# Cutting the 576 result columns of three products at column 252 instead of 288, and laying them as one run over two PSUM banks

## The chip, the core and the metric

The kernel runs on one core of a Trainium2 chip. The metric is the device time of one execution in microseconds, lower is better. A core has five engines that work side by side: PE (TensorE: matmuls; its loading of the stationary operand has a row of its own, PEld), DVE (VectorE), ACT (ScalarE), POOL (GpSimd) and SP (SyncE, which here only starts DMAs). PE writes its results to PSUM, a memory of eight banks, each with 512 fp32 columns on 128 partitions. A matmul's results lie within one bank, so 576 columns need at least two matmuls.

## What is computed

Two kinds of block alternate, each twice, over 2048 rows of 576 values: a linear attention, then a layer of 64 experts that each of 32 heads chooses from. Each adds to its input.

```python
x = x + _A_ref(_layernorm(x, axis=-1), A_wqkv, A_wo)
x = x + _B_ref(_layernorm(x, axis=-1), B_w_q, B_k1, B_k2, B_u, B_v)
x = x + _A_ref(_layernorm(x, axis=-1), A_wqkv, A_wo)
x = x + _B_ref(_layernorm(x, axis=-1), B_w_q, B_k1, B_k2, B_u, B_v)
```

`_A_ref` makes q, k and v (`x @ wqkv`, 576 columns each, 32 heads of 18), takes phi(t) = t + 1 for t > 0, else exp(t), plus 1e-6, of q and k, sums phi(k) times v over all rows for each head, multiplies phi(q) with that sum, divides by phi(q) times the sum of phi(k), and multiplies with `wo`. `_B_ref` scores every row for 32 heads against two sets of 8 keys, takes the best of each (one of 64 experts), weighs that expert's row of `v` with the gelu of x times its row of `u`, and sums over the heads.

## The kernel before

**Tiles and layers.** The 2048 rows are 16 tiles of 128. For each of the two layers a *front* makes k, v, q and the state (the sum over all tiles), and a *back* makes the attention's output, the scores, the choice and the experts' output, tile by tile. The back of a tile of layer 0 runs beside the front of an earlier tile of layer 1.

**Precision.** A product in float32r loses low bits, so each operand is split in a high and a low part (`split`, L102; names ending in hi and lo), and a product is the sum of hi x hi, hi x lo and lo x hi. With 576 = 4.5 x 128 contraction rows in five blocks, that is 14 passes (`passes`, L48). Each pass takes two matmuls, one for each part of the 576 result columns: 28 matmuls for one product of a tile.

**The products that the change concerns.**
- `product` (L207, matmul L214) makes k, v and q of a tile: tiles ppk, ppv, ppq. A PSUM tile is 1024 columns, two banks. k and q are cut at `HALF` = 288: columns 0 to 287 go to the first bank from its head, 288 to 575 to the head of the second (column 512). v alone passes `cut=2 * HC` = 252, so that whole groups of seven heads (126 columns) lie together; its parts are 252 and 324 wide, each at the head of a bank.
- `back_out` (L403, matmul L410) makes the attention's output, ppo: 14 passes of two 288-wide matmuls (`out_passes`, L329).
- `exp_out` (L516, matmul L525) makes the experts' output, po: two passes, four matmuls. In the last layer three tiles (10, 11 and 12) begin with an identity matmul that puts the residual into PSUM (`exp_base`, L509, L514).

**Who reads them.** `phi` (L218) reads ppk and ppq twice: exp on ACT (L220) and a max-and-add on DVE (L223), with an in-place step on DVE between them (L221). `residual` (L396, L399) adds ppo or po to the input on DVE and sums the row. For the three tiles with an identity matmul ACT copies po instead (L530). All of them see the two parts through `halves` (L69), a view of 2 x 288 columns with a step of 512.

**Order.** Within `in_order(...)` (L144) the instructions of PE, ACT, DVE and POOL keep the order in which the code issues them, engine by engine. That order is written by hand: a loop over tiles for layer 0's front (L703 on), then lists of pieces (`play`, L674; L760, L779) and a step that is repeated eight times (`step2`, L680). In a list `k1.10` is the next part of layer 1's k for tile 10, `q` and `lq` the q products, `O` the output product, `S` the scores, `po` the experts' output, `sel` the choice on DVE. PSUM tiles come from a ring of four (L66).

Of the kernel before, what the change touches and what calls it, by code (L numbers as in the profile page):

```python
# [15 lines left out]
AF = mybir.ActivationFunctionType  # L16
ALU = mybir.AluOpType
# [4 lines left out]
S, D, H, DH = 2048, 576, 32, 18  # L22
# [2 lines left out]
DK, E, NE = 128, 8, 64  # L25
HC = 7 * DH
HALF = D // 2
EPS_LN = 1e-5
EPS = 1e-6
GELU_C = float(np.sqrt(2.0 / np.pi))  # L30
# [8 lines left out]
def blocks(rem):  # L39

    rows, at = [], 0
    for b in range(NB):
        rows.append((at, b - (b > rem)))
        at += 64 if b == rem else P
    return rows


def passes(rem):  # L48
    rest = [b for b in range(NB) if b != rem]
    return ([("hi", b, "hi") for b in range(NB)] + [("hi", b, "lo") for b in rest]  # L50
            + [("lo", b, "hi") for b in range(NB)])


REM, REM_O = 2, 4
# [3 lines left out]
def network(ctx, tc, x_in, wqkv, wo, wq_t, k_t, u_t, v2, c_mask, c_mask4, c_ident, c_code, c_code1, c_scale, c_shift, out):  # L58
    nc = tc.nc
# [6 lines left out]
    def psum(name):  # L66
        return ps.tile([P, 1024], F32, tag="ps", name=name)

    def halves(t):  # L69
        return t.rearrange("p (b c) -> p b c", b=2)[:, :, :HALF]  # L70


    ident = cp.tile([P, P], F32, name="ident")
# [10 lines left out]
    whi = cp.tile([P, NB, 3 * D], F32R, name="whi")  # L84
    wlo = cp.tile([P, 4, 3 * D], F32R, name="wlo")
# [4 lines left out]
    vmix = cp.tile([P, D], F32R, name="vmix")  # L90
# [67 lines left out]
    def statistics(xt, n, soon=False):  # L158
        st = wk.tile([P, 2, 6], F32, tag="st", name=f"st{n}")
        nc.vector.bn_stats(st[:, 0], xt[:, :HALF])  # L160
        nc.vector.bn_stats(st[:, 1], xt[:, HALF:])
        mv = wk.tile([P, 2], F32, tag="mv", name=f"mv{n}")
        nc.vector.bn_aggr(mv, st.rearrange("p a b -> p (a b)"))  # L163
        rs = wk.tile([P, 2], F32, tag="rs", name=f"rs{n}")
        nc.gpsimd.tensor_scalar(rs[:, 0:1], mv[:, 1:2], EPS_LN, 1.0, op0=ALU.add, op1=ALU.mult)  # L165
        nc.gpsimd.tensor_tensor(rs[:, 0:1], rs[:, 0:1], mhalf, op=ALU.pow)
# [4 lines left out]
    def spread(xt, total, n):  # L171

        m = wk.tile([P, 2], F32, tag="mv", name=f"m{n}")
        nc.gpsimd.tensor_scalar(m[:, 0:1], total, -1.0 / D, 1.0, op0=ALU.mult, op1=ALU.mult)  # L174
        nc.scalar.activation(junk, xt, AF.Square, bias=m[:, 0:1], accum_out=m[:, 1:2])  # L175
        return m

    def layernorm_sum(xt, m, n):
        rs = wk.tile([P, 2], F32, tag="rs", name=f"rs{n}")
        nc.gpsimd.tensor_scalar(rs[:, 0:1], m[:, 1:2], 1.0 / D, EPS_LN, op0=ALU.mult, op1=ALU.add)  # L180
        nc.gpsimd.tensor_tensor(rs[:, 0:1], rs[:, 0:1], mhalf, op=ALU.pow)
        nc.gpsimd.tensor_tensor(rs[:, 1:2], m[:, 0:1], rs[:, 0:1], op=ALU.mult)  # L182
        return normalized(xt, rs, n)
# [20 lines left out]
        split(pt[:, :w], hi.rearrange("p a b -> p (a b)")[:, :w], lo.rearrange("p a b -> p (a b)")[:, :w])  # L204
        return hi, lo

    def product(tt, hi, lo, cols, n, cut=HALF, rem=REM, by_block=False):  # L207

        o = psum(f"pp{n}")
        todo = sorted(passes(rem), key=lambda p: p[1]) if by_block else passes(rem)  # L210
        for i, (a, b, w) in enumerate(todo):
            wb = hi[:, b] if w == "hi" else lo[:, blocks(rem)[b][1]]
            for c0, c1, at in ((0, cut, 0), (cut, D, 512)):
                nc.tensor.matmul(o[:, at:at + c1 - c0], tt[a == "lo"][:, b, :], wb[:, cols + c0:cols + c1],  # L214
                                 start=(i == 0), stop=(i == len(todo) - 1))
        return o

    def phi(p, n):  # L218
        e = wk.tile([P, D], F32, tag="e", name=f"e{n}", bufs=4)
        nc.scalar.activation(e.rearrange("p (b c) -> p b c", b=2), halves(p), AF.Exp)  # L220
        nc.vector.tensor_scalar(e, e, 1.0, EPS, op0=ALU.min, op1=ALU.add)  # L221
        e2 = e.rearrange("p (b c) -> p b c", b=2)
        nc.vector.scalar_tensor_tensor(e2, halves(p), 0.0, e2, op0=ALU.max, op1=ALU.add)  # L223
        return e

    tt = {}
# [9 lines left out]
    def front_k(l, t):  # L236
        k = product(tt["f", l, t], whi, wlo, D, f"k{l}_{t}", by_block=(l == 0 and t == 0))
        yield
        tt["fk", l, t] = phi(k, f"k{l}_{t}")

    def front_v(l, t):
        v = product(tt["f", l, t], whi, wlo, 2 * D, f"v{l}_{t}", cut=2 * HC)
        yield
        vt = v5[t % 2]
        for c, x in ((0, v[:, :2 * HC]), (4, v[:, 512:512 + 2 * HC])):
            nc.scalar.activation(vt[:, c:c + 4, :63], x.rearrange("p (c e) -> p c e", c=4), AF.Copy)  # L246
        yield
        nc.scalar.activation(vt[:, 8:, :36], v[:, 512 + 2 * HC:512 + 2 * HC + 72].rearrange("p (c e) -> p c e", c=2), AF.Copy)

    def front_q(l, t):  # L250
        q = product(tt["f", l, t], whi, wlo, 0, f"q{l}_{t}")
        yield
        fq = phi(q, f"q{l}_{t}")
        nc.sync.dma_start(pq_d[l][t], fq)
# [74 lines left out]
    def out_passes():  # L329
        todo = [(0, b, ohi[:, b], HC if b < 4 else P) for b in range(NB)]  # L330
        todo += [(0, b, olo[:, b], HC) for b in range(4)]
        todo += [(1, b, ohi[:, b], HC) for b in range(4)]
        return todo + [(1, 4, olo[:, 4], 112)]

    def state_fold(l, b):
# [3 lines left out]
        for h in range(2):  # L339
            nc.tensor.matmul(m[:c, h * 512:h * 512 + HALF], kvb[:n, b * HC:b * HC + c], wob[l][b][:n, h * HALF:(h + 1) * HALF],  # L340
                             start=True, stop=True)
# [54 lines left out]
    def residual(p, xt, n, tag):  # L396
        y = wk.tile([P, D], F32, tag=tag, name=f"{tag}{n}", bufs=BUFS[tag])
        total = wk.tile([P, 1], F32, tag="sum", name=f"sum{tag}{n}")
        nc.vector.scalar_tensor_tensor(y.rearrange("p (b c) -> p b c", b=2), halves(p), 0.0,  # L399
                                       xt.rearrange("p (b c) -> p b c", b=2), op0=ALU.add, op1=ALU.add, accum_out=total)  # L400
        return y, total

    def back_out(l, t):  # L403
        n = f"{l}_{t}"
        hl = tt.pop(("oT", l, t))
        p = psum("ppo" + n)
        todo = sorted(out_passes(), key=lambda x: x[1]) if t == 0 else out_passes()
        for i, (a, b, w, r) in enumerate(todo):
            for h in range(2):
                nc.tensor.matmul(p[:, h * 512:h * 512 + HALF], hl[a][:r, b], w[:r, h * HALF:(h + 1) * HALF],  # L410
                                 start=(i == 0), stop=(i == len(todo) - 1))
        yield
        x1, total = residual(p, xs.pop(("a", l, t)), n, "x1")
        xs["b", l, t] = x1
        yield
        m = spread(x1, total, "b" + n)
        yield
        ys["b", l, t] = layernorm_sum(x1, m, "b" + n)
# [90 lines left out]
    def exp_base(l, t):  # L509

        p = tt["base", l, t] = psum(f"po{l}_{t}")
        x1 = xs.pop(("b", l, t))
        for b in range(2):
            nc.tensor.matmul(p[:, b * 512:b * 512 + HALF], ident, x1[:, b * HALF:(b + 1) * HALF], start=True, stop=False)  # L514

    def exp_out(l, t):  # L516
        n = f"{l}_{t}"
        c = tt.pop(("c", l, t))
        p = tt.pop(("base", l, t), None)
        based = p is not None  # L520
        if not based:
            p = psum("po" + n)
        for i in range(2):
            for b in range(2):
                nc.tensor.matmul(p[:, b * 512:b * 512 + HALF], c[i], vmix[:, b * HALF:(b + 1) * HALF],  # L525
                                 start=(i == 0 and not based), stop=(i == 1))
        yield
        if based:
            x2 = wk.tile([P, D], F32, tag="x2", name=f"x2{n}", bufs=BUFS["x2"])
            nc.scalar.activation(x2.rearrange("p (b c) -> p b c", b=2), halves(p), AF.Copy)  # L530
        else:
            x2, total = residual(p, xs.pop(("b", l, t)), n, "x2")
        if l == 0:
            nc.sync.dma_start(x_d[t], x2)
            yield
            m = spread(x2, total, "f" + n)
            yield
            ys["f", 1, t] = layernorm_sum(x2, m, "f" + n)
        else:
            nc.sync.dma_start(out[t * P:(t + 1) * P, :], x2)  # L540
# [125 lines left out]
    keep, rl, lq, ldx, ldq = front_keep, late_load, late_q, back_x, back_pq  # L666
    fl, ln, lv, sv = first_load, first_ln, load_vu, split_vu
    k, v, q, fT, st = front_k, front_v, front_q, front_T, front_state
    wl, mk, zs, M = wo_load, state_mask, state_sum, state_fold
    ld, num, oT, O = back_load, back_scale, back_oT, back_out  # L670
# [32 lines left out]
    with in_order(*ALL):  # L703
        x0, x1 = xs.pop(("f", 0)), xs.pop(("f", 1))
# [156 lines left out]
```

## Time and profile before

| what | value |
|---|---|
| runs | 750.99, 752.0 and 753.03 us; median 752.0 |
| profiled execution | span of 750.2 us from the first instruction to the last; what lies around the span is not in it, and no other time is given for this execution |
| PE | 731.1 us busy, 5672 matmuls |
| PEld | 681.5 us, as many weight loads |
| DVE | 460.1 us |
| ACT | 289.6 us |
| POOL | 197.5 us |
| granted TensorE clock | 0.996 of full speed on the mean |
| HBM | 55.12 MB read, 23.56 MB written, 105 GB/s over the span |

A matmul's row in the profile spans from its start to its modelled end, and one begins before the one ahead has ended. So the cost of a matmul in a stream is read from the distance between starts, not from its length. A row such as `41.83 1.46 PE L214 MATMUL ppv<-whi,thif ... x10` of the timeline is ten matmuls, merged, the first of which starts 41.83 us after the span's start. In the busy table of stretches, each engine has its busy time and the number of its instructions; behind them stand the granted clock, the share of the DMA engines and GB/s.

### The profile page before, as it was taken

The numbers are of one execution on the slowest core, as the hardware profiler recorded it, in microseconds if no ns is written. First come the engines' busy times: TensorE is split into PE (matmuls) and PEld (weight loads), VectorE is DVE, ScalarE is ACT, GpSimd is POOL, SyncE is SP. The second block draws the span as 40 slices with busy tenths as digits, with TensorE's granted clock in tenths as the row PEclk, the third lists the DMA queues.
The fourth block names the chain that finished last, engine by engine and source line by source line (L and its number), as shares of the span: only waits on it lengthen the run. The fifth ranks groups of instructions, "written<-read, shape, count | busy, mean of one in ns | idle before, by whom it ended". The sixth has DMA issues, their size and how long they took to land. (4 is left out here: it accounts for less than half of the span.)

```text
span 750.2 us, 14647 instructions
## 1 busy us (share of the span) xinstructions
PE 731.1 (97%) x5672; PEld 681.5 (91%) x5672; DVE 460.1 (61%) x1006; ACT 289.6 (39%) x588; POOL 197.5 (26%) x541
## 2 busy tenths in 40 slices
PE   7999999999999999999999999999999999999995
PEld 5999989999998889999999999999899999999984
DVE  4632342324236886666666666563366899899986
ACT  4422232232324544444444444452233333444343
POOL 2110001001003543333333333130033334533431
PEclk9999999999999999999999999999999999999999
DMA  9726446631120322222222212222624323121101
GB/s 267 253 98 235 175 165 227 223 118 50 48 64 32 111 99 71 95 85 90 102 103 88 83 69 86 80 71 68 176 87 119 103 83 116 31 87 41 48 33 64
DMA packets 52471, 79.64 MB, mean 106 GB/s; under 512 B 5617, under 2 KB 22513, under 8 KB 52401
## 3 DMA queue, kind: packets, MB, share of 16 engines
q1 hardware_dynamic: 52400, 78.70, 32.0%
q8 instruction: 45, 0.74, 0.4%
q14 instruction: 26, 0.20, 0.1%
HBM read 55.12 MB, written 23.56 MB: 105 GB/s over the span
## 5 line engine op out<-in xcount | busy, mean ns | idle before, releaser
L221 DVE TENSOR_SCALAR ek<-ek 128x576 f32<-128x576 f32 x32 | 15.1, 472 | 81.7 <-ACT ek L220 81.7
L214 PE MATMUL ppk<-whi,thif 128*128 128x288 f32 x320 | 51.0, 304 | 2.3 <-ACT thif L104 2.2
L214 PEld LDWEIGHTS ppk<-whi,thif 128*128 128x128 f32 x320 | 44.9, 191 | 6.7 <-issue 3.3
L410 PE MATMUL ppo<-ohi,thio 126*128 126x288 f32 (+1 forms) x320 | 50.7, 301 | 0.1
L214 PE MATMUL ppk<-whi,tlof 128*128 128x288 f32 x320 | 49.2, 299 | 0.3 <-DVE tlof L105 0.3
L165 POOL TENSOR_SCALAR rsf<-mvf 128x1 f32<-128x1 f32 x16 | 3.1, 192 | 173.4 <-DVE mvf L163 173.3
L221 DVE TENSOR_SCALAR eq<-eq 128x576 f32<-128x576 f32 x32 | 15.6, 489 | 53.8 <-ACT eq L220 53.8
L214 PE MATMUL ppv<-whi,thif 128*128 128x252 f32 x320 | 47.4, 295 | 0.1
L214 PE MATMUL ppv<-whi,tlof 128*128 128x252 f32 x320 | 46.9, 293 | 0.0
L189 ACT ACTIVATE yb<-x,rsb 128x640 f32<-128x640 f32 x32 | 29.6, 923 | 43.4 <-POOL rsb L182 43.3
L441 PE MATMUL pps<-shi,thib 128*128 128x512 f32 x160 | 43.9, 404 | 2.0 <-ACT thib L104 2.0
L214 PEld LDWEIGHTS ppk<-whi,tlof 128*128 128x128 f32 x320 | 45.4, 191 | 0.5 <-DVE tlof L105 0.5
L410 PEld LDWEIGHTS ppo<-ohi,thio 126*128 126x128 f32 (+1 forms) x320 | 44.9, 189 | 1.0 <-DVE eq L223 0.3
L214 PEld LDWEIGHTS ppv<-whi,thif 128*128 128x128 f32 x320 | 43.7, 188 | 0.4 <-ACT thif L104 0.3
L214 PEld LDWEIGHTS ppv<-whi,tlof 128*128 128x128 f32 x320 | 43.9, 188 | 0.0
L175 ACT ACTIVATE junk<-x,mb 128x576 bf16<-128x576 f32 x32 | 24.7, 771 | 49.6 <-POOL mb L174 46.3
L441 PE MATMUL pps<-shi,tlob 128*128 128x512 f32 x160 | 42.7, 397 | 0.0
L246 ACT ACTIVATE v<-ppv 128x252 f32<-128x252 f32 x64 | 20.9, 378 | 53.3 <-PE ppv L214 53.3
L214 PE MATMUL ppq<-whi 128*128 128x288 f32 x260 | 39.8, 299 | 0.6 <-DVE eq L223 0.6
L214 PE MATMUL ppk<-wlo,thif 128*128 128x288 f32 x256 | 40.3, 299 | 0.0
L410 PE MATMUL ppo<-olo,thio 126*128 126x288 f32 x256 | 40.3, 296 | 0.0
L410 PE MATMUL ppo<-ohi,tloo 126*128 126x288 f32 x256 | 40.3, 296 | 0.0
(155 smaller groups left out, 1749.0 us busy)
## 6 DMA issues: line engine op xcount, KB each, us to landing
fold<-in_wq_t SPq DMA_DIRECT2D x64, 288.0 KB, 5.0
whi<-hl_d SPq DMA_DIRECT2D x26, 320.0 KB, 3.1
pq_d<-eq SPq DMA_DIRECT2D x19, 288.0 KB, 2.1
pq<-pq_d SPq DMA_DIRECT2D x19, 288.0 KB, 2.9
xf<-in_x SPq DMA_DIRECT2D x16, 288.0 KB
x<-in_x SPq DMA_DIRECT2D x16, 288.0 KB, 2.7
x_d<-x SPq DMA_DIRECT2D x16, 288.0 KB, 3.2
x<-x_d SPq DMA_DIRECT2D x16, 288.0 KB, 2.7
```

The costliest lines, as they stand in the source:

```text
L165: nc.gpsimd.tensor_scalar(rs[:, 0:1], mv[:, 1:2], EPS_LN, 1.0, op0=ALU.add, op1=ALU.mult)
L175: nc.scalar.activation(junk, xt, AF.Square, bias=m[:, 0:1], accum_out=m[:, 1:2])
L189: nc.scalar.activation(y, x2, AF.Identity, scale=rs[:, 0:1], bias=rs[:, 1:2])
L214: nc.tensor.matmul(o[:, at:at + c1 - c0], tt[a == "lo"][:, b, :], wb[:, cols + c0:cols + c1], start=(i == 0), stop=(i == len(todo) - 1))
L221: nc.vector.tensor_scalar(e, e, 1.0, EPS, op0=ALU.min, op1=ALU.add)
L246: nc.scalar.activation(vt[:, c:c + 4, :63], x.rearrange("p (c e) -> p c e", c=4), AF.Copy)
L410: nc.tensor.matmul(p[:, h * 512:h * 512 + HALF], hl[a][:r, b], w[:r, h * HALF:(h + 1) * HALF], start=(i == 0), stop=(i == len(todo) - 1))
L441: nc.tensor.matmul(p[:, :512], hl[a == "lo"][:, b, :], shi[:, b] if w == "hi" else slo[:, blocks(REM)[b][1]], start=(i == 0), stop=(i == l ...
```

## The change

The parts of k, q, the output product and the experts' output become columns 0 to 251 and 252 to 575, as v's are. The first part is put at columns 260 to 511 of the PSUM tile, at the end of the first bank, and the second at 512, the head of the second bank. So the 576 results are one run from column 260 to 835, and the readers take them as one flat run (`row`) instead of two. v keeps its places (0 and 512). The number of matmuls, weight loads, reads and DMAs and their order on each engine are as before.

```diff
+CUT = 2 * HC
...
+    def row(t):
+        return t[:, 512 - CUT:512 - CUT + D]
+
+    PARTS = (0, CUT, 512 - CUT), (CUT, D, 512)
...
-    def product(tt, hi, lo, cols, n, cut=HALF, rem=REM, by_block=False):
+    def product(tt, hi, lo, cols, n, parts=PARTS, rem=REM, by_block=False):
...
-            for c0, c1, at in ((0, cut, 0), (cut, D, 512)):
+            for c0, c1, at in parts:
                 nc.tensor.matmul(o[:, at:at + c1 - c0], tt[a == "lo"][:, b, :], wb[:, cols + c0:cols + c1],
                                  start=(i == 0), stop=(i == len(todo) - 1))
...
-        nc.scalar.activation(e.rearrange("p (b c) -> p b c", b=2), halves(p), AF.Exp)
+        nc.scalar.activation(e, row(p), AF.Exp)
         nc.vector.tensor_scalar(e, e, 1.0, EPS, op0=ALU.min, op1=ALU.add)
-        e2 = e.rearrange("p (b c) -> p b c", b=2)
-        nc.vector.scalar_tensor_tensor(e2, halves(p), 0.0, e2, op0=ALU.max, op1=ALU.add)
+        nc.vector.scalar_tensor_tensor(e, row(p), 0.0, e, op0=ALU.max, op1=ALU.add)
...
-        v = product(tt["f", l, t], whi, wlo, 2 * D, f"v{l}_{t}", cut=2 * HC)
+        v = product(tt["f", l, t], whi, wlo, 2 * D, f"v{l}_{t}", parts=((0, CUT, 0), (CUT, D, 512)))
...
-        nc.vector.scalar_tensor_tensor(y.rearrange("p (b c) -> p b c", b=2), halves(p), 0.0,
-                                       xt.rearrange("p (b c) -> p b c", b=2), op0=ALU.add, op1=ALU.add, accum_out=total)
+        nc.vector.scalar_tensor_tensor(y, row(p), 0.0, xt, op0=ALU.add, op1=ALU.add, accum_out=total)
...
-            for h in range(2):
-                nc.tensor.matmul(p[:, h * 512:h * 512 + HALF], hl[a][:r, b], w[:r, h * HALF:(h + 1) * HALF],
-                                 start=(i == 0), stop=(i == len(todo) - 1))
+            for c0, c1, at in PARTS:
+                nc.tensor.matmul(p[:, at:at + c1 - c0], hl[a][:r, b], w[:r, c0:c1], start=(i == 0), stop=(i == len(todo) - 1))
...
-        for b in range(2):
-            nc.tensor.matmul(p[:, b * 512:b * 512 + HALF], ident, x1[:, b * HALF:(b + 1) * HALF], start=True, stop=False)
+        for c0, c1, at in PARTS:
+            nc.tensor.matmul(p[:, at:at + c1 - c0], ident, x1[:, c0:c1], start=True, stop=False)
...
-            for b in range(2):
-                nc.tensor.matmul(p[:, b * 512:b * 512 + HALF], c[i], vmix[:, b * HALF:(b + 1) * HALF],
-                                 start=(i == 0 and not based), stop=(i == 1))
+            for c0, c1, at in PARTS:
+                nc.tensor.matmul(p[:, at:at + c1 - c0], c[i], vmix[:, c0:c1], start=(i == 0 and not based), stop=(i == 1))
...
-            nc.scalar.activation(x2.rearrange("p (b c) -> p b c", b=2), halves(p), AF.Copy)
+            nc.scalar.activation(x2, row(p), AF.Copy)
```

## The prediction

> **What bounds the kernel now.** First the head of the page, sections 1 and 2: busy time by engine, then busy tenths in 40 slices, with the TensorE clock that was granted.
>
> ```profile
> span 750.2 us, 14647 instructions
> PE 731.1 (97%) x5672; PEld 681.5 (91%) x5672; DVE 460.1 (61%) x1006; ACT 289.6 (39%) x588; POOL 197.5 (26%) x541
> ...
> PE   7999999999999999999999999999999999999995
> ...
> DVE  4632342324236886666666666563366899899986
> ...
> PEclk9999999999999999999999999999999999999999
> ```
>
> TensorE has work in every slice and full clock in all; VectorE is half idle early and close to full in the last ten slices. The matmul ends are modelled, so a busy PE alone doesn't show a PE at its limit. The question is where it ever waits, and who else is full there. The busy table over five stretches (columns: stretch, its length, then busy us and instruction count of PE, PEld, DVE, ACT, POOL):
>
> ```profile
> 20.00:240.00 220.00, 218.86 (x1986) 205.33 (x1986) 83.76 (x166) 68.74 (x154) 21.78 (x56) 1.00 0.42 142
> 240.00:320.00 80.00, 77.72 (x574) 72.14 (x573) 60.50 (x134) 38.46 (x78) 32.23 (x87) 1.00 0.26 88
> 320.00:540.00 220.00, 218.33 (x1714) 207.02 (x1713) 129.24 (x292) 91.35 (x190) 59.90 (x178) 1.00 0.29 94
> 540.00:640.00 100.00, 99.19 (x688) 94.15 (x687) 80.05 (x160) 35.81 (x67) 38.62 (x93) 1.00 0.31 95
> 640.00:751.00 111.00, 101.74 (x643) 91.66 (x641) 96.89 (x239) 44.69 (x88) 40.49 (x116) 0.99 0.15 52
> ```
>
> From 20 to 240 and from 320 to 540 PE is idle 1.1 and 1.7 us of 220, with DVE at 38% and 59%: there PE alone sets the pace. From 240 to 320 it waits 2.3 us for others. After 640 DVE is busy 96.9 of 111 us, nearly as long as PE.
>
> What does a PE instruction cost there? Its duration is no help, since matmuls overlap; the distance from one start to the next is. The timeline of PE around 40 us (start, length, engine, line, operation, shape, count) shows a k, a v and a q product back to back, with no wait between:
>
> ```profile
> 40.50 1.50 PE L214 MATMUL ppk<-whi,tlof 128*128 128x288 f32 x10
> 41.83 1.46 PE L214 MATMUL ppv<-whi,thif 128*128 128x252 f32 x10
> 43.13 1.20 PE L214 MATMUL ppv<-wlo,thif 128*128 128x252 f32 x8
> 44.17 1.46 PE L214 MATMUL ppv<-whi,tlof 128*128 128x252 f32 x10
> 45.47 1.49 PE L214 MATMUL ppq<-whi,thif 128*128 128x288 f32 x10
> 46.80 1.23 PE L214 MATMUL ppq<-wlo,thif 128*128 128x288 f32 x8
> 47.87 1.49 PE L214 MATMUL ppq<-whi,tlof 128*128 128x288 f32 x10
> 49.20 0.71 PE L199 MATMUL ptf<-ident,yf 128*128 128x128 f32 x5
> 49.84 0.81 PE L286 MATMUL kva<-ek,v 128*64 128x72 f32 x20
> ```
>
> All three have 28 matmuls, the same 576 result columns and the same stationary tiles. v (252 and 324 columns by turns; the row names the first shape) takes 45.47 - 41.83 = 3.64 us, q (288 and 288) 49.20 - 45.47 = 3.73. The last ten of k take 1.33, so 28 take 3.72. v is 0.09 us cheaper: 130 ns a matmul where k and q have 133. That is the measurement that the forecast stands on: the kernel holds its own comparison of the two cuts, at the same clock, a microsecond apart. The stationary tiles being warm from k isn't the reason, since q comes after v on the same tiles and is slow again.
>
> **The change part by part.** *Matmuls.* It neither adds nor removes an instruction or a DMA, and the order on no engine moves; only shapes and places change. The products concerned are k, q and the output product: 32 each (16 tiles, two layers), 96 in all, 28 matmuls each. If each takes v's pace, k and q win 0.09 each. For the output product the chain of work that ended last gives whole products:
>
> ```profile
> 639.77 0.77 DVE x L399 x2
> ...
> 651.50 0.33 PE ptb L199
> 651.83 3.75 PE ppo L410 x28
> 655.58 0.54 PE po L525 x4
> ...
> 697.45 0.75 DVE x L399 x2
> ...
> 704.96 1.62 DVE o L387
> ...
> 706.71 0.74 PE pto L199 x5
> ```
>
> 3.75 against 3.64 is 0.11. That makes 64 x 0.09 + 32 x 0.11 = 9.3 us. The expert output has four matmuls in 0.54 us, 135 ns each; at v's 130 it wins 0.02 for each of 32 tiles, 0.6 us. The three tiles that begin with an identity matmul gain nothing by it that a row shows. All of PE is 9.9 us, the ceiling.
>
> *What of it reaches the end.* The busy table by tile (columns as above) tells where the products lie, 28 matmuls each. k, where it stands in 240 to 320; behind that no other stretch is needed, since none is left after 540:
>
> ```profile
> 240.00:320.00 80.00, 11.87 (x84) 11.37 (x84) 2.27 (x3) 1.93 (x3) 1.00 0.26 88
> ```
>
> q, and then the output product, in 240 to 320 and after 540:
>
> ```profile
> 240.00:320.00 80.00, 3.98 (x28) 3.77 (x28) 1.51 (x2) 1.27 (x2) 1.00 0.26 88
> ...
> 540.00:751.00 211.00, 55.42 (x392) 52.79 (x392) 10.61 (x14) 9.02 (x14) 0.99 0.23 72
> ```
>
> ```profile
> 240.00:320.00 80.00, 21.63 (x155) 20.65 (x153) 4.57 (x12) 1.00 0.26 88
> ...
> 540.00:751.00 211.00, 63.38 (x448) 60.64 (x448) 12.17 (x32) 0.99 0.23 72
> ```
>
> So 3 + 1 + 5.5 = 9.5 products lie in 240 to 320, and 14 + 16 = 30 after 540. The other 56 (10 of them output products) lie before 240 and in 320 to 540; the very first k, in the start-up, is left out.
> - The 56 stand where PE hardly waits: 46 x 0.09 + 10 x 0.11 = 5.2 us, all of it earned, and 0.3 for 13 expert outputs.
> - 240 to 320: 4 x 0.09 + 5.5 x 0.11 = 1.0. PE's 2.3 us of waits there are for others, and between two such waits a faster PE only waits longer, unless the chain that it waits for began on PE. I take half, 0.5.
> - After 540: 14 x 0.09 + 16 x 0.11 + 16 x 0.02 = 3.3. In the chain above, the stretches from 639.77 to 651.50 and from 697.45 to 706.71 run on DVE; the one between is PE's. On DVE's stretches the gain is lost, on PE's it counts until DVE is late. I take half, 1.6.
>
> The sum is 5.5 + 0.5 + 1.6 = 7.6 us.
>
> *Reads.* phi, the residual and the last copy now read 576 results as one run over a bank's end, where they read two runs of 288. Both kinds of read are in the trace (shapes, then busy, mean ns):
>
> ```profile
> L105 DVE TENSOR_TENSOR tloo<-pto,thio 128x640 fp32r<-128x640 f32 x32 | 26.3, 820 | 12.7 <-ACT thio L104 12.7
> L105 DVE TENSOR_TENSOR tlob<-ptb,thib 128x768 fp32r<-128x768 f32 x27 | 25.8, 955 | 8.1 <-ACT thib L104 8.1
> L399 DVE SCALAR_TENSOR_TENSOR x<-ppo,x 128x576 f32<-128x576 f32 x32 | 24.1, 754 | 11.5 <-PE ppo L410 9.5 <-DMA x<-x_d 1.7 <-POOL g L460 0.2
> L325 ACT ACTIVATE zb<-z 128x576 f32<-128x576 f32 x2 | 1.3, 651 | 4.6 <-PE z L323 4.6
> L530 ACT ACTIVATE x<-po 128x576 f32<-128x576 f32 x3 | 2.0, 651 | 2.7 <-PE po L525 2.7
> ```
>
> On DVE flat reads of 640 and 768 over the bank's end give 135 ns per 128 columns, so 576 would be 820 - 67 = 753, against 754 for the two runs. On ACT the flat copy zb and the two-run copy x both take 651. I cost this at nothing; 2 ns on 125 DVE reads would be 0.25 us either way, and only after 640 would it be felt.
>
> *Where the results are put.* What v does not show is the new place: its 252 begin at a bank's head, the new ones at column 260. Nearest rows on one side: the five transposes at 49.20 write at columns 0, 128, 256, 384 and 512 and take 0.64 us together, 128 ns each, no step to be seen. On the other: the sums of the state (z) begin at column 8 and leave holes, and are slower than the fold that follows:
>
> ```profile
> 226.69 0.72 PE L322 MATMUL z<-zc,pick 128*128 128x288 f32 x2 [0.63 <-ACT zc L305]
> 227.25 0.31 PE L323 MATMUL z<-zc,pick 128*128 128x36 f32 x2
> 227.98 3.15 PE L340 MATMUL m<-wob,kvb 127*126 127x288 f32 x12
> 230.76 1.71 PE L214 MATMUL ppq<-whi,thif 128*128 128x288 f32 x10
> ```
>
> z: 0.56 us for two, 280 ns each; m: 2.78 for twelve, 232 each. The 48 ns hold a cold start after a wait and a strided source too, so they bound the price of an odd column from above. From below it is nothing; a gain over v's pace has no row. I take nothing, the transposes being plain dense writes as these are.
>
> *A rule against it.* The trace has 133 and 130 ns a matmul. The Trainium skill, page "TensorE: Matmul & The Clock Gate", section "Back-to-back issue gap", gives for single matmuls at full clock the columns over 2.4 GHz plus about 2.5 ns. By that both cuts cost 245 ns a pair and the change would be worth 0; the rows, at 266 and 260, contradict it for this operand type.
>
> **How that stands to the time.** The profiled span is 750.2, the median of the runs 752.0 (1.8 more). What is saved lies inside the span, so it comes off the median: 752.0 - 7.6 = **744.4 us**.
>
> **The rivals.**
> - *All or nothing late.* If DVE never becomes the limit, the ceiling: 752.0 - 9.9 = 742.1. If DVE and ACT eat all of it in both weak stretches: 752.0 - 5.5 = 746.5. Both are the same mechanism and belong to the forecast's case.
> - *The pace isn't the cut's.* The 0.09 may be owed to where v stands in the bank, its two results both at a bank's head. Then at column 260 a pair takes 266 as now, the change doesn't do what it says, and the time is 752.0. For it: no row has an odd cut at another place. Against: q and k begin at the head as well and are slow.
> - *Writes from column 260 are dear.* One matmul of each pair starts off a bank's head. If that costs p ns, a pair wins 6.5 - p, so from p = 6.5 on the change loses. With 13 ns (what a 288 takes over the 120 of 2.4 GHz, once more) 1376 pairs lose 6.5 ns each, 8.9 us, on an engine that has no slack: about 761. The z rows speak for it, the transposes against it.
>
> **How the numbers follow.** The cut sets the pace: 0.79, 742.1 to 746.5 at 744.4, with tails to 741.2 (the runs shown differ by 1 us from their median) and 749. No change: 0.13, 750.5 to 753.5. Dear writes: 0.08, above 754.3. To leave out no more than 2 in 10 the range takes in the first case and the near edge of the second: 741.2 to 751.0. A measurement of this kernel can tell about 0.3% (2.3 us) from no change: faster 0.79, same 0.13, slower 0.08.
>
> **What would show it.** In the new trace, a k, v and q product in a row should start 3.64 us apart, all three; the PE stretch before 240 should be some 2.7 us shorter; PE's waits in the last fifth should have grown by about the 1.6 us that is lost there, ended by DVE or ACT; the reads should keep 754 and about 645 ns. If q and k still take 3.73, the pace was not the cut's. If they take more, the place is dear. If they take 3.64 and the span is shorter by much less than 5 us, another engine paces stretches that I gave to PE.

## The result

The changed kernel takes 747.2 us (745.96 to 748.71), the one before 751.7 in the same session (750.99 to 753.03): ratio 0.9943, 95% interval 0.9926 to 0.9961. The forecast was 744.4 in a range of 741.2 to 751.0. So the change makes the kernel faster, by 4.5 us where 7.6 were expected. The page of the changed kernel:

```profile
span 746.9 us, 14647 instructions
...
PE 726.5 (97%) x5672; PEld 675.2 (90%) x5672; DVE 458.9 (61%) x1006; ACT 289.7 (39%) x588; POOL 200.4 (27%) x541
...
PE   7999999999999999999999999999999999999995
...
DVE  3732332324236887666666666563366899999986
...
PEclk9999999999999999999999999999999999999998
```

The span is 3.3 us shorter and PE 4.6 us less busy; DVE, ACT and POOL are within 3 us of what they were. First the forecast's own test: a k, a v and a q product in a row. The timeline of PE in the changed kernel (start, length, then the instructions):

```profile
39.45 1.46 PE L220 MATMUL ppk<-whi,thif 128*128 128x252 f32 x10
...
43.09 1.46 PE L220 MATMUL ppv<-whi,thif 128*128 128x252 f32 x10
...
46.73 1.46 PE L220 MATMUL ppq<-whi,thif 128*128 128x252 f32 x10
...
50.38 0.71 PE L205 MATMUL ptf<-ident,yf 128*128 128x128 f32 x5
```

3.64, 3.64 and 3.65 us: k and q now run at v's pace, from column 260 of the bank as from its head. The readers of the output products on DVE and of the last expert outputs on ACT are as they were (754 and 651 ns before), and so are those of k and q (758 ns on DVE, 642 and 647 on ACT, before and after):

```profile
L404 DVE SCALAR_TENSOR_TENSOR x<-ppo,x 128x576 f32<-128x576 f32 x32 | 24.1, 754 | 10.4 <-PE ppo L414 7.2 <-DMA x<-x_d 1.8
```

```profile
L532 ACT ACTIVATE x<-po 128x576 f32<-128x576 f32 x3 | 2.0, 651 | 2.9 <-PE po L528 2.9
```

So the mechanism is right and the sum is too large. Where the rest went shows when the same instructions are compared by their starts. Four marks in the kernel before: the second and the third k product, the first late q product that waits for DVE, and the last matmuls of the last expert output.

```profile
16.91 1.60 PE L214 MATMUL ppk<-whi,thif 128*128 128x288 f32 x10 [0.79 <-ACT thif L104]
...
38.10 1.50 PE L214 MATMUL ppk<-whi,thif 128*128 128x288 f32 x10
...
547.84 1.58 PE L214 MATMUL ppq<-whi 128*128 128x288 f32 x10 [0.59 <-DVE eq L223]
...
745.99 0.49 PE L525 MATMUL po<-vmix,tlob 128*128 128x288 f32 x2
```

And in the changed one, whose third k product stands above, at 39.45:

```profile
18.44 1.32 PE L220 MATMUL ppk<-whi,thif 128*128 128x252 f32 x8 [0.79 <-ACT thif L110]
...
545.69 1.60 PE L220 MATMUL ppq<-whi 128*128 128x252 f32 x10 [0.61 <-DVE eq L228]
...
742.69 0.55 PE L528 MATMUL po<-vmix,tlob 128*128 128x252 f32 x2
```

Up to the second k it is 1.5 us *later*; from there to that q it wins 530.93 - 527.25 = 3.7 us; from there to the end 198.15 - 197.00 = 1.15. From the third k, where the start-up is over, to that q it wins 509.74 - 506.24 = 3.5. The forecast had 6.0 and 1.6 for the two stretches, and nothing for the start.

### The profile page after: what moved, and what is told of

The parts are those of the page before. It is cut to its first block, busy times and chain, and to the rows that moved or that the text cites. A ratio compares the mean times of both kernels' runs of the same rounds, so it can differ in the third digit from the quotient of the medians.

```text
span 746.9 us, 14647 instructions
## 1 busy us (share of the span) xinstructions
PE 726.5 (97%) x5672; PEld 675.2 (90%) x5672; DVE 458.9 (61%) x1006; ACT 289.7 (39%) x588; POOL 200.4 (27%) x541
## 4 chain that ended last, share of the span: by engine, by line
PE 82%; DVE 10%; ACT 3%; issue 2%; POOL 1%; DMA 1%; SPq 0%; DVEq 0%; POOLq 0%; ACTq 0%
PE ppk L220 15%; PE ppv L220 15%; PE ppq L220 13%; PE ppo L414 13%; PE pps L444 12%; PE kva L291 3%; PE fold_ps L560 2%; PE ptb L205 2%; PE ptf L205 2%; PE pto L205 2%; PE po L528 2%; DMA wst<-in_wqkv 1%; PE m L345 1%; DVE o L392 1%; DVE tlob L111 1%
## 5 line engine op out<-in xcount | busy, mean ns | idle before, releaser
L220 PE MATMUL ppk<-whi,thif 128*128 128x252 f32 x320 | 50.3, 302 | 2.4 <-ACT thif L110 2.3
L414 PE MATMUL ppo<-ohi,thio 126*128 126x252 f32 (+1 forms) x320 | 50.2, 299 | 0.1
L220 PE MATMUL ppk<-whi,tlof 128*128 128x252 f32 x320 | 48.2, 295 | 0.3 <-DVE tlof L111 0.3
L449 ACT ACTIVATE s<-pps 128x512 f32<-128x512 f32 x32 | 19.1, 596 | 54.9 <-PE pps L444 54.9
L220 PE MATMUL ppq<-whi 128*128 128x252 f32 (+1 forms) x260 | 39.6, 299 | 0.6 <-DVE eq L228 0.6
L404 DVE SCALAR_TENSOR_TENSOR x<-po,x 128x576 f32<-128x576 f32 x29 | 21.9, 753 | 29.3 <-PE po L528 28.3
L414 PE MATMUL ppo<-olo,thio 126*128 126x252 f32 (+1 forms) x256 | 39.5, 293 | 0.0
```

Of the source, the lines that this page charges most:

```text
L404: nc.vector.scalar_tensor_tensor(y, row(p), 0.0, xt, op0=ALU.add, op1=ALU.add, accum_out=total)
L414: nc.tensor.matmul(p[:, at:at + c1 - c0], hl[a][:r, b], w[:r, c0:c1], start=(i == 0), stop=(i == len(todo) - 1))
L449: nc.scalar.activation(s[:, NE:], p[:, :512], AF.Copy)
```

## The experiments

All kernels here compute the whole result. Each is timed in five rounds against the kernel before on its own chip; "pair" is the distance from one 252 (or other first part) to the next in a stream.

**The changed kernel again.**

> The changed kernel once more, unaltered, timed against the one before on this chip in more rounds. In its first profile the first warm-up and weight-load stretch (to 20 us) came out 1.45 us later than in the profile before, with the same instructions. Theory 1, chance of the start: here the delay at 20 us comes out differently (anything from -1.5 to 1.5), and the ratio of the runs stays at 0.993 to 0.996. Rival, the new cut makes the first k product dearer at its half clock: the 1.4 us are there again.

747.26 us against 751.01, ratio 0.9946 (0.9932 to 0.996). Its second k product starts 0.3 us behind that of the profile of before, not 1.5, and in the other kernels below it starts 0.4 to 1.4 us ahead, the two with a cut of 240 and 216 among them. From 10 to 17 us the granted clock was 0.76 in the profiles of before, of the changed kernel and of this repeat, and 1.00 in all the others, which the page's slices, 9 throughout, don't show; in those three, pairs of the first k product are 480 ns apart for some microseconds. So the late start was chance. From the second to the third k product the repeat takes 21.7 us where the changed kernel took 21.0 with the same instructions, so that stretch varies by chance too. From the third k product to the late q the repeat takes 506.2 us again and wins 3.5; from there to the end it wins 0.9, not 1.15. Differences below some 0.3 us in that last stretch can't be told from chance.

**Placement and flat reading alone.**

```diff
-CUT = 2 * HC
+CUT = 288
```

(v keeps its own cut of 252 here and in the other kernels with a changed `CUT`.)

> The placement and the flat reading alone, with the old cut: columns 0 to 287 at 224 to 511 of the PSUM tile, 288 to 575 at 512. Theory 1, the widths alone set the pace: k, q and the output product keep 266 ns a pair, the time is that of before within 0.5 us (ratio 0.9995 to 1.0005), reads within 5 ns. Rival, place or flat reading have a part in it: pairs nearer to 260, or reads faster, and half of the gain or more (ratio under 0.997).

750.82 against 751.01, ratio 0.9998 (0.9989 to 1.0006). A q product in its stream, from its first matmul to the transposes behind it:

```profile
44.56 1.50 PE L220 MATMUL ppq<-whi,thif 128*128 128x288 f32 x10
...
48.28 0.71 PE L205 MATMUL ptf<-ident,yf 128*128 128x128 f32 x5
```

3.72 us, where before has 3.73. Laying the results as one run and reading them flat is worth nothing and costs nothing, to within the interval's 0.8 us. So the gain is the widths'.

**The same widths, the long one first.**

```diff
-CUT = 2 * HC
+CUT = 324
```

> The same two widths in the other order: 324 columns first, at 188 to 511, then 252. Theory 1, the pair of widths sets the pace: 260 ns a pair in a stream, the ratio to before as that of the changed kernel within 0.1%. Rival, it is the short one going first that matters (its weight load being hidden by the 324 ahead of it): another pace, 266 or more. After a product the next one starts 146 ns behind a 324 and 114 behind a 252, so this order should win 32 ns for each product that something else than a product follows, if the next instruction needs no longer.

```profile
44.00 1.48 PE L220 MATMUL ppq<-whi,thif 128*128 128x324 f32 x10
...
47.68 0.71 PE L205 MATMUL ptf<-ident,yf 128*128 128x128 f32 x5
```

747.62 us, ratio 0.9961 (0.9946 to 0.9975). The pair takes 259 to 268 ns in the early products, 263 on the mean, not 260: the order has a part in it, so neither theory holds as it was put. In the late q products the order is the better one: 3.74 us on the mean of 15, where the short part first has 3.77, which makes up 0.5 us. The 32 ns for each product that were expected besides can't be seen: in a stream a product still takes its 14 pairs from its start to the start of what follows. The intervals of the two orders overlap.

**Other cuts**, 256, 240, 216 and 264, each by one number in `CUT`.

> A cut four columns further: 256 and 320. In the trace before, the widths 128, 288 and 512 (all multiples of 32) take 13 to 20 ns more than their columns over 2.4 GHz, and 252 and 324 take 9 to 11. Theory 1a, multiples of 32 (or 16) are what is slow: 266 ns a pair or more, time as before (751.5). Theory 1b, only unequal widths matter, the short one's excess being covered by the long one: 260 a pair, time as with 252 (747.2).

> The cut twelve columns earlier: 240 and 336. The 256 and 320 of the run before came to 264 ns a pair, between 260 and 267, so neither of its two theories held. Theory 4, the short matmul may be as short as the weight load beside it allows, about 109 ns (the transposes' pace): 240 columns take 100 ns plus some 10, and the pair stays at 260; time as the changed kernel within 0.1%. Rival, only 252 is good, by its own rhythm: 264 or more, time 748 to 751.

> A cut well below: 216 and 360. Theory 4: 216 columns take 90 ns, less than the 109 of a weight load, so the short one is held up to 109 or more and the pair comes to 109 + 161 = 270 ns or more; 1376 pairs by 3 to 4 ns over before, time 751 to 756. Rival, the weight load is hidden under the long matmul ahead: 260 a pair still, time as the changed kernel.

> The cut twelve columns later: 264 and 312. So far a pair takes 273 ns with 216, 267 with 240, 260 with 252, 264 with 256 and 267 with 288. Theory 5, 252 lies in a narrow dip and beyond it the pair goes back to 288's pace: 264 to 267 ns, time 748 to 751. Rival, 256 is the odd one and the range from 252 to 288 is uneven: 262 or less, time 745 to 747.5.

The same two rows of each, 256 first, then 240, 216 and 264:

```profile
44.43 1.48 PE L220 MATMUL ppq<-whi,thif 128*128 128x256 f32 x10
...
48.12 0.71 PE L205 MATMUL ptf<-ident,yf 128*128 128x128 f32 x5
```

```profile
43.83 1.50 PE L220 MATMUL ppq<-whi,thif 128*128 128x240 f32 x10
...
47.56 0.71 PE L205 MATMUL ptf<-ident,yf 128*128 128x128 f32 x5
```

```profile
45.57 1.53 PE L220 MATMUL ppq<-whi,thif 128*128 128x216 f32 x10
...
49.40 0.71 PE L205 MATMUL ptf<-ident,yf 128*128 128x128 f32 x5
```

```profile
44.14 1.50 PE L220 MATMUL ppq<-whi,thif 128*128 128x264 f32 x10
...
47.87 0.71 PE L205 MATMUL ptf<-ident,yf 128*128 128x128 f32 x5
```

The ratio is estimated over all runs, so it need not be the quotient of the medians.

| first part | a q product in its stream | time, ratio to before (interval) |
|---|---|---|
| 216 | 3.83 us | 760.98 us, 1.0127 (1.0113 to 1.0141) |
| 240 | 3.73 | 751.58, 1.0004 (0.9995 to 1.0013) |
| 252 | 3.65 | 747.26, 0.9946 (0.9932 to 0.996) |
| 256 | 3.69 | 748.86, 0.9983 (0.997 to 0.9996) |
| 264 | 3.73 | 750.07, 0.9995 (0.9986 to 1.0004) |
| 288 | 3.72 | 750.82, 0.9998 (0.9989 to 1.0006) |
| 324 | 3.68 | 747.62, 0.9961 (0.9946 to 0.9975) |

252 lies in a narrow dip. Theory 1a falls (256 and 320 are multiples of 32 and faster than 288), and so does 1b (240 and 336 are unequal and as slow as 288). Theory 4 fails at 240, where it has 260 ns and the pair takes 267. At 216 its price is met: 270 ns or more, measured 273. There the weight loads start 107 to 109 and 164 to 170 ns apart by turns in the q product above (the matmuls 97 to 103 and 171 to 180), and in no profile of this case do two weight loads of one product start less than 107 ns apart. So the short part keeps to the load's pace here, which is theory 4's reason. With 252 the loads are 115 and 145 ns apart, so there that pace is not the limit. The time of 216 is above theory 4's 751 to 756 because the pair is 7 ns over 288's 267, not 3 to 4. What holds for the rest is theory 5, for the early products, and that is a description. Why 252 and 324 fit, the runs don't tell.

**Early products alone, late products alone.** The cut is chosen by layer and stage:

```diff
+    EARLY, LATE = CUT, HALF
...
-            for c0, c1, at in PARTS:
+            for c0, c1, at in parts_of(LATE if l else EARLY):
```

> The new cut for everything that runs before 540 us (k, the early q, the first layer's output products and expert outputs), the old cut of 288 for the second layer's late q, output products and expert outputs. Theory 1, the late part is half lost to DVE: from 20 to 540 us PE comes 3.6 to 3.8 us further ahead of the kernel before, as with the whole change, and stays there; ratio 0.9945 to 0.9960 against 0.9946 for the whole change. Rival, the late part is earned as the early one: the ratio is 0.9965 or above.

> The complement: the old cut until 540 us, the new one for the second layer's late q, output products and expert outputs. Theory 1: 30 products that win 0.03 (q) and 0.07 us (output) each make 1.5 us of PE, of which DVE lets through about 1.2 at most; ratio 0.998 to 0.9995. Rival, all late work is paid in full at 0.09 or more a product: 2.7 us, ratio 0.9965.

Early alone: 747.0 us, ratio 0.9939 (0.9926 to 0.9952). Late alone: 750.6, 0.9988 (0.9976 to 0.9999). The early kernel's third k product, late q and last matmuls:

```profile
37.29 1.46 PE L224 MATMUL ppk<-whi,thif 128*128 128x252 f32 x10
...
543.42 1.58 PE L224 MATMUL ppq<-whi 128*128 128x288 f32 x10 [0.59 <-DVE eq L232]
...
741.49 0.50 PE L533 MATMUL po<-vmix,tlob 128*128 128x288 f32 x2
```

From the third k to the late q it takes 506.13 us and wins 3.6, as the whole change does (3.5 twice). From its late q to its last mark it takes 198.07 us, against 198.15 before: the early gain arrives whole at the end, nothing is given back behind it. The late kernel wins 1.2 us on that stretch, where the whole change wins 1.15 and its repeat 0.9. The times don't tell the whole change from its early part, since a microsecond is within their intervals; the rows do. Theory 1 is met in both parts, though the early ratio lies just under its range. Its reason is only half right: the starts of all products after 540 us add up to 1.5 us less PE, of which 0.9 to 1.2 arrive, so 0.3 to 0.6 us are kept back there, less than half.

**A wait taken away.** In the repeated step, the last part of the normalization (`num`) goes behind the split of the transposed tile:

```diff
-        run(0, (num, s + 2))
+        run(0, (num, s + 2, 1))
         run(1, (v, s - 3, 1))
-        run(0, (bc, (s, s - 1)))
+        run(0, (bc, (s, s - 1)), (num, s + 2))
```

> The whole change, and in the repeated step of the middle the last part of the attention's normalization (reciprocal, product, on DVE) is issued behind the split of the transposed tile instead of ahead of it. In the changed kernel PE waits there, once a step, for DVE's split before the scores (1.5 us in 7 times by PEld). Theory 2, the faster products took the slack of that split, and it is late only for what stands ahead of it on DVE: the waits go, the transposes of the output (pto) take 19.4 us in the sum again instead of 20.3, and the time is 0.5 to 0.9 us under the changed kernel. Rival, the wait is only handed on to another one in the step: time as the changed kernel.

The table of waits from 320 to 500 us (total us, times, longest) has a row in the changed kernel that is not there in the kernel before:

```profile
PEld pps L444 <- DVE tlob L111: 1.5, 7, 0.2
```

The table leaves out idle times under 0.15 us. Its timeline in one step, DVE's product o ahead of the split tlob, and the weight load of the scores pps, 50 ns after the split's end:

```profile
335.41 0.76 DVE L392 TENSOR_TENSOR o<-pq,r 128x576 f32<-128x576 f32 x1
...
336.08 0.95 DVE L111 TENSOR_TENSOR tlob<-ptb,thib 128x768 fp32r<-128x768 f32 x1
...
337.08 1.00 PEld L444 LDWEIGHTS pps<-shi,thib 128*128 128x128 f32 x5 [0.21 <-DVE tlob L111]
```

The same two in the kernel before:

```profile
337.10 0.96 DVE L105 TENSOR_TENSOR tlob<-ptb,thib 128x768 fp32r<-128x768 f32 x1 [0.15 <-ACT thib L104]
...
338.11 0.99 PEld L441 LDWEIGHTS pps<-shi,thib 128*128 128x128 f32 x5
```

The scores' first matmul reads only thib, which is ready earlier. By the code its PSUM tile comes from the ring of four, where the split still reads ptb; that this is what holds it is inferred, no run shows it apart. With the order changed:

```profile
334.04 0.96 DVE L111 TENSOR_TENSOR tlob<-ptb,thib 128x768 fp32r<-128x768 f32 x1 [1.29 <-ACT thib L110]
...
335.06 1.00 PEld L444 LDWEIGHTS pps<-shi,thib 128*128 128x128 f32 x5
...
335.29 0.76 DVE L392 TENSOR_TENSOR o<-pq,r 128x576 f32<-128x576 f32 x1
```

The row of waits is gone. The distance from the split's end to the load stays: it is 52 to 55 ns in each of these steps in all three kernels, so the split sets the scores' start in each of them. What differs is how long PE's loader has been idle by then: 0.10 us before, 0.21 with the change, and 0.10 again with the order changed. Five steps, from one output product to the sixth, take 88.73 us before:

```profile
342.02 1.50 PE L410 MATMUL ppo<-ohi,thio 126*128 126x288 f32 x10
...
430.75 1.49 PE L410 MATMUL ppo<-ohi,thio 126*128 126x288 f32 x10
```

88.46 with the change:

```profile
341.01 1.48 PE L414 MATMUL ppo<-ohi,thio 126*128 126x252 f32 x10
...
429.47 1.48 PE L414 MATMUL ppo<-ohi,thio 126*128 126x252 f32 x10
```

and 87.92 with the split moved:

```profile
338.98 1.47 PE L414 MATMUL ppo<-ohi,thio 126*128 126x252 f32 x10
...
426.90 1.48 PE L414 MATMUL ppo<-ohi,thio 126*128 126x252 f32 x10
```

A step's k and output product win 0.17 us, of which 0.05 came through and 0.16 do now. From 328 to 473 us the changed kernel and its repeat win 0.53 us each, the two kernels with the split moved (this one and the last one below) 1.3 each. The time is 746.48 us, ratio 0.9934 (0.9918 to 0.9949): better by these rows, though the times alone don't set it apart from the changed kernel. Theory 2 holds (pto takes 19.5 us in the sum where it has 19.4), except that there was next to no slack to take.

**The late q's stationary tiles.** The late q products win less than the others. In the changed kernel the starts of their matmuls are 112, 148, 117 and 150 ns apart by turns, where the early ones have 114 and 146. Two theories on the place of the tiles:

```diff
-    whi = cp.tile([P, NB, 3 * D], F32R, name="whi")
+    whi = cp.tile([P, NB, 1792], F32R, name="whi")
...
-        at = (1 + t // 2 % 2) * D + t % 2 * 2 * P
+        at = 640 + t // 2 % 2 * 4 * P + t % 2 * 2 * P
```

> The whole change, and the stationary tiles that the late q products read are put at multiples of 512 bytes: the rows of the weight tile get 1792 columns instead of 1728, and the tiles begin at column 640. In the changed kernel the late q has 112, 148, 117 and 150 ns by turns, period two blocks, where the blocks are 6912 bytes apart (13.5 times 512). Theory 3, the place of the stationary tile in its 512 bytes costs the 7 ns of every second pair: the late q comes to 114 and 146 throughout, its 13 products win another 0.03 to 0.05 us each, 0.5 us on PE, and the time is 0 to 0.5 us under the changed kernel. Rival, it is the tile that is shared with the moving operand: the pattern stays.

```diff
-    whi = cp.tile([P, NB, 3 * D], F32R, name="whi")
+    whi = cp.tile([P, NB, D + 10 * P], F32R, name="whi")
...
+        own = whi[:, t % 4, D:].rearrange("p (a b c) -> p a b c", a=2, b=NB)
+        hi, lo = own[:, 0], own[:, 1]
```

> The kernel with the split ahead of the normalization (as in the run before that moved it), and the stationary tiles of the late q laid with their five blocks side by side, 512 bytes apart, as the tiles of the early products have them, but still in the tile that also holds the moving weights. Theory 3b, the distance between successive stationary blocks sets the late q's pace: 114 and 146 throughout, its 13 products win 0.04 us more each (0.5 us of PE), and the time is 0 to 0.5 us under the kernel with the split moved. Rival, the shared tile does it: 112, 148, 117 and 150 stay. Either way the split that was moved keeps its 0.5 to 0.9 us against the changed kernel, so the ratio to before is 0.992 to 0.994.

746.0 us (ratio 0.9932, 0.992 to 0.9945) and 746.61 (0.9936, 0.9923 to 0.9948). In both the 112, 148, 117 and 150 are unchanged, so neither the multiple of 512 bytes nor the distance of the blocks makes them: theories 3 and 3b fall. That the tile shared with the moving operand does it is what remains of the rivals, but no run put the stationary in a tile of its own, so it isn't shown. The lower time of the first can't come from its late q, which takes 3.77 us on the mean as in the changed kernel; its runs overlap those of that kernel, and its profile started 1.0 us ahead of the one before, a stretch that the first experiment showed to vary by chance. The second, which has the split moved too, has a wait of its own: one late q product waits 1.5 us for the DMA of its stationary tiles, so its time is not a measure of the late q alone.

## Why the prediction was right, and its sum too large

**Right:** the engine that sets the pace; that the pace is the cut's and can be read off v; that column 260 costs nothing (k and v both 3.64 us) and the flat reads neither (placement alone: 0.9998); that the stretches before 240 us hand their gain to the end (from 38 to 238 us 2.1 us are won on the three products and 1.9 arrive). The two rivals that would have held the time at 752 or raised it to 761 are out. The 747.2 us lie beyond the 742.1 to 746.5 of the main case, in the tail to 749 that it was given. By the formula for single matmuls of the Trainium skill, page "TensorE: Matmul & The Clock Gate", section "Back-to-back issue gap", both cuts of the 576 columns would cost the same; the trace and the seven cuts above disagree with it for this stream of float32r matmuls, each with its own weight load.

**The step that failed is the size of one product's gain:** "64 x 0.09 + 32 x 0.11 = 9.3 us", and with it "The expert output ... wins 0.02 for each of 32 tiles, 0.6 us". Summed from the start of each product to the start of what follows, k went from 123.3 to 120.8 us, q from 122.1 to 120.4, the output product from 121.3 to 119.1: 6.4 us, 0.067 each. The expert output went from 23.6 to 23.7: nothing. Of the 2.9 us that the three products fall short, 1.3 are the output product's, 0.9 the late q's and 0.7 those of k and the early q. Two things are in it, and a third kept back a part of what was won.

*Most products don't run in a stream.* A k product behind the fold, first before, then after the change (the second row is the start of what follows):

```profile
52.70 1.60 PE L214 MATMUL ppk<-whi,thif 128*128 128x288 f32 x10
...
56.53 0.68 PE L214 MATMUL ppv<-whi,thif 128*128 128x252 f32 x4
```

```profile
53.87 1.58 PE L220 MATMUL ppk<-whi,thif 128*128 128x252 f32 x10
...
57.63 0.54 PE L220 MATMUL ppv<-whi,thif 128*128 128x252 f32 x3
```

3.83 and 3.76: 0.07. The first distance is some 200 ns or more instead of 114 or 133, and one to three of the pairs behind it run at 265 to 272 with either cut. Some 57 of the 96 start like that. The output product's "3.75" was one of them, and was held against a v in full stream: its 0.11 mixed the start with the cut. Nor was it a distance between starts, since the chain's pieces begin and end with the modelled ends; by starts that product takes 3.84:

```profile
651.58 1.59 PE L410 MATMUL ppo<-ohi,thio 126*128 126x288 f32 x10
...
655.42 0.43 PE L525 MATMUL po<-vmix,thib 128*128 128x288 f32 x2
```

In the middle steps, in a stream, it went from 3.74 to 3.67: 0.08. The expert output has only two pairs and never reaches its pace. (The rival with dear writes counts 1376 pairs; with two for each expert output they are 1408, which moves its 761 by 0.2.)

*The late q has its own pace.* One of them, before and after:

```profile
547.84 1.58 PE L214 MATMUL ppq<-whi 128*128 128x288 f32 x10 [0.59 <-DVE eq L223]
...
551.66 0.43 PE L410 MATMUL ppo<-ohi,thio 126*128 126x288 f32 x2
```

```profile
545.69 1.60 PE L220 MATMUL ppq<-whi 128*128 128x252 f32 x10 [0.61 <-DVE eq L228]
...
549.49 0.43 PE L414 MATMUL ppo<-ohi,thio 126*128 126x252 f32 x2
```

3.82 and 3.80: 0.02 here, 0.03 on the mean of the 15 late ones, where 0.09 was taken from v.

*"The 56 stand where PE hardly waits: ... all of it earned"* holds before 240 us and fails from 328 to 473, where 1.36 us were won on the three products and 0.53 arrived. The tables showed no wait there, but already before the change the split ended 0.05 us ahead of the scores' first weight load (338.06 and 338.11), as close as where PE waits for it, and the loader had been idle for 0.10 us: there was no slack behind a PE that looked full, and the forecast had not looked for it. Of the 0.17 us a step, 0.11 went into that wait. Between the two stretches, from 238 to 328 us, 0.7 us were won and 0.5 arrived, where the forecast had 1.0 and 0.5.

The late stretch came near in size by two errors that offset each other, which is luck: 3.3 us of PE with half lost was the forecast, 1.5 us with 0.3 to 0.6 lost is what there was. PE's waits behind 540 us, which were to grow by about 1.6 us, grew by some 0.4 (from 5.23 to 5.68 us, counting those over 0.15).

## What to carry to other kernels

When a kernel holds the same work in two shapes, the distance between starts in its own trace is a better price than any formula, but compare like with like: in a stream with in a stream, behind a wait with behind a wait, and count how many are of each kind. An engine that seems never to idle can still be about to wait, or wait for less than a table of waits lists: before a gain is booked as earned, look up how long ahead of need each of its inputs, and each of its PSUM buffers, comes free. And try the neighbours of a good size: here four columns more lost half of what a product gains (3.69 us, between 3.65 and 3.72).

## What the runs showed of the hardware

Two float32r matmuls that share 576 columns, each with its own weight load, took 260 ns at 252 and 324, 264 at 256 and 320, 266 to 267 at 240, 264 and 288, and 273 at 216, in early k and q products in a stream. The same 252 and 324 took 263 on the mean in the other order. The best cut was another one for the late q, whose stationary tiles lie elsewhere: from its fifth pair on it had 263 at 252, but 261 with 324 first and 261 at 264. Two weight loads of one product never started less than 107 ns apart. A product written from column 260 of a bank took what v takes at a bank's head (3.64 us), and a read of one run over a bank's end what two runs within banks take (754 ns on DVE, 651 on ACT).
